# Bias of a two-layer kernel on Trainium2: column sums of w_out split between GpSimd and TensorE, one eviction of the result

## The chip, the cores and the metric

One core of a Trainium2 chip. The time is the device time of an execution in microseconds (us); executions of a kernel are compared with the executions of the kernel before in the same rounds on the same chip. Engines in the profile: PE is TensorE's matmuls, PEld its weight loads, DVE is VectorE, ACT is ScalarE, POOL is GpSimd, SP is SyncE.

## The reference

A spectral mixing layer (real FFT along 3008 positions, a complex 256x256 product with soft threshold, inverse FFT), then a two-layer network on 24064 tokens of width 256 with 2048 hidden units:

```python
h = x @ w_in
r = np.maximum(h, 0.0)
g = s * (r * r) + b
return (g @ w_out).astype(np.float32)
```

Since s and b are scalars, g @ w_out = s * (r*r @ w_out) + b * (column sums of w_out). Those column sums times b are the "bias": 256 numbers, wanted on all 128 partitions.

## The kernel before

It loads w_out as 16 blocks of 128 x 256 in f16 (one DMA from GpSimd's queue), adds the blocks two at a time on GpSimd in f32, folds the two halves, lets TensorE sum over the partitions with a matrix of ones, and lets ScalarE multiply by b and evict the result from PSUM twice, into the two halves of `bias_bc`:

```python
w_out_t = cpool.tile([P, MC, D], F16, name="w_out_t")
bias_bc = cpool.tile([P, 2, D], F32, name="bias_bc")
# ... cut
def sum_w_out():
    acc = opool.tile([P, 2, D], F32, name="acc", tag="ost")
    nc.gpsimd.tensor_tensor(out=acc, in0=w_out_t[:, 0:2], in1=w_out_t[:, 2:4], op=ALU.add)
    for q in range(4, MC, 2):
        nc.gpsimd.tensor_tensor(out=acc, in0=acc, in1=w_out_t[:, q : q + 2], op=ALU.add)
    nc.gpsimd.tensor_tensor(out=w_sum, in0=acc[:, 0], in1=acc[:, 1], op=ALU.add)

def make_bias():
    ps = other_bank()
    nc.tensor.matmul(ps[:, 0:D], ones, w_sum, start=True, stop=True)
    for j in range(2):
        nc.scalar.activation(out=bias_bc[:, j], in_=ps[:, 0:D], func=AF.Copy, scale=bb_bc)
```

The stage that runs meanwhile, and all the rest of the kernel, is this loop: first-stage products into two double banks `psh` (line 769), relu by ScalarE into `rt` (776), square mostly by VectorE into `gt` (783), second-stage products into `psa` (840), eviction with s and the bias by VectorE (850).

```python
nc.tensor.matmul(o, w_in_t[dc][:, mc * P : (mc + 1) * P], r, ...)              # 769
nc.scalar.activation(out=rt[:, :, 0:w], in_=ps[:, :, 0:w], func=AF.Relu)       # 776
nc.vector.tensor_tensor(out=gt[:, :, 0:w], in0=rt[:, :, 0:w], in1=rt[:, :, 0:w], op=ALU.mult)
nc.tensor.matmul(ps[0:size, h, :], gts[...][:, mc % 2, ...], w_out_t[:, mc, :], ...)   # 840
nc.vector.scalar_tensor_tensor(
    out=ost[0:size, 0:k], in0=ps[0:size, 0:k], scalar=s_bc[0:size],
    in1=bias_bc[0:size, 0:k], op0=ALU.mult, op1=ALU.add)                       # 850
# ... cut
plan.setdefault(15, []).append(make_bias)   # slot 15 of the first output tile
```

The framework that builds the kernel orders each engine's instructions by its own schedule, so a slot is a priority rather than a place.

## Time and profile before

| | before |
|---|---|
| median time | 847.02 us (3 runs, 846.86 to 847.43) |
| TensorE busy | 833.8 us, 99% of the span of 845.0 |
| VectorE, ScalarE, GpSimd busy | 82%, 76%, 5% |
| bias matmul at / w_sum ready at | 51.95 us / 50.0 us |
| TensorE's true idle time from 48 to 60 us, after 60 us | 0.84 us, 4.9 us |

How to read it: the busy share counts a matmul as busy for its whole latency (0.27 us for the bias matmul, whose successor starts 0.11 us after it), so it hides short waits. The last row is the idle time that the prediction works out from the matmuls' starts; it is what a smoother schedule could win.

### The profile page before, as it was taken

How to read it: one execution, taken by the hardware profiler on the slowest of the kernel's cores; microseconds unless marked ns; L12 is line 12 of the kernel's file. 1: busy time of each engine (PE TensorE's matmuls, PEld its weight loads, DVE VectorE, ACT ScalarE, POOL GpSimd, SP SyncE). 2: the span in 40 equal slices, each digit the busy share in tenths (PEclk: the TensorE clock that was granted, in tenths of full speed). 3: DMA queues.
4: the chain of work that ended last, by engine and by line, in shares of the span. 5: the costliest groups of instructions: out<-in, count | busy, mean ns of one | idle time of the engine just before them, and what ended most of it. 6: DMA issues, size and time to landing. Idle time of an engine off the chain costs nothing.

```text
span 845.0 us, 17114 instructions
## 1 busy us (share of the span) xinstructions
PE 833.8 (99%) x6653; PEld 599.6 (71%) x6653; DVE 693.6 (82%) x1026; ACT 641.8 (76%) x864; POOL 45.0 (5%) x71
## 2 busy tenths in 40 slices
PE   8999999999999999999999999999999999999997
PEld 6857767777677766777677776777667777766765
DVE  5989987888888987888888888798978888776674
ACT  5988887778778877787777787778877878766673
POOL 5331000000000001000000000000000000000000
PEclk9999999999999999999999999999999999999999
DMA  8945567124752367324761248513354223411111
GB/s 202 180 143 122 121 173 203 57 77 101 203 154 56 101 169 190 92 68 107 189 175 49 81 103 205 160 42 91 113 144 125 64 74 95 112 33 38 38 44 50
DMA packets 105746, 96.06 MB, mean 114 GB/s; under 512 B 9542, under 2 KB 97482, under 8 KB 104322
## 3 DMA queue, kind: packets, MB, share of 16 engines
q1 hardware_dynamic: 99218, 80.55, 33.0%
q0 software_dynamic: 6448, 14.42, 10.6%
q8 instruction: 52, 0.85, 0.4%
q14 instruction: 28, 0.23, 0.1%
HBM read 53.52 MB, written 46.66 MB: 119 GB/s over the span
## 4 chain that ended last, share of the span: by engine, by line
PE 90%; ACT 3%; DMA 3%; DVE 2%; issue 1%; POOL 0%; SPq 0%; ACTq 0%; DVEq 0%; POOLq 0%
PE psa L840 37%; PE psh L769 36%; PE psf L635 4%; PE psf L570 2%; PE psf L621 2%; PE psf L606 2%; PE psf L665 2%; PE psf L718 2%; ACT rt L776 2%; PE psm L426 1%; DMA x<-in_x_dram 1%; DMA ud<-u 1%; DVE gt L783 1%; DMA us<-ud 1%; DMA F_c<-dft_fwd 0%
## 5 line engine op out<-in xcount | busy, mean ns | idle before, releaser
L776 ACT ACTIVATE rt<-psh 128x1024 f32<-128x1024 f32 (+2 forms) x384 | 386.7, 1008 | 119.6 <-PE psh L769 117.5
L783 DVE TENSOR_TENSOR gt<-rt 128x1024 f16<-128x1024 f32 (+2 forms) x322 | 385.7, 1202 | 95.4 <-ACT rt L776 94.5
L840 PE MATMUL psa<-w_out_t,gt 128*128 128x256 f16 (+1 forms) x3024 | 454.4, 272 | 0.1
L840 PEld LDWEIGHTS <-gt 128*128 128x128 f16 (+1 forms) x3024 | 300.9, 101 | 187.0 <-issue 1.4
L769 PE MATMUL psh<-yt,w_in 128*128 128x512 f16 (+1 forms) x1344 | 396.3, 378 | 0.2 <-ACT rt L776 0.2
L769 PEld LDWEIGHTS <-w_in 128*128 128x128 f16 x1536 | 142.8, 98 | 27.3 <-issue 1.8
L850 DVE SCALAR_TENSOR_TENSOR ost<-psa,s_bc,bias_bc 128x512 f32<-128x512 f32 (+2 forms) x97 | 71.1, 733 | 10.0 <-PE psa L840 8.2
L780 ACT ACTIVATE gt<-rt 128x1024 f16<-128x1024 f32 (+2 forms) x62 | 65.3, 1054 | 1.0
L640 DVE TENSOR_TENSOR ring<-psf,s 128x512 f16<-128x512 f32 x84 | 57.5, 685 | 3.8 <-PE psf L635 3.3
L170 ACT CAST v<-psf 128x512 f16<-128x512 f32 x78 | 45.3, 583 | 19.7 <-PE psf L665 19.7
L170 ACT CAST xf<-psf 128x512 f16<-128x512 f32 x82 | 47.9, 586 | 10.9 <-PE psf L606 10.9
L170 ACT CAST u<-psf 96x512 f16<-96x512 f32 x76 | 43.9, 580 | 12.4 <-PE psf L570 12.2
L769 PE MATMUL psh<-tail,w_in 128*128 128x512 f16 (+1 forms) x192 | 52.1, 353 | 0.0
L635 PE MATMUL psf<-W_g,xf 128*128 128x256 f16 x336 | 50.4, 273 | 0.0
L170 ACT CAST yt<-psf 128x480 f16<-128x480 f32 (+2 forms) x73 | 37.8, 525 | 11.6 <-PE psf L718 11.6
L213 POOL DMA_DIRECT2D x<-in_x_dram x36 | 18.7, 526 | 430.3 <-PE psf L570 429.2
L570 PE MATMUL psf<-x,A_t 94*96 94x512 f16 x103 | 39.3, 382 | 1.1 <-ACT yt L170 0.5
L646 DVE TENSOR_TENSOR ring<-ring,high 128x512 f16<-128x512 f16 x84 | 35.6, 423 | 2.3
L647 DVE TENSOR_TENSOR ring<-ring 128x512 f16<-128x512 f16 x84 | 35.5, 423 | 2.0
L645 DVE TENSOR_TENSOR ring<-ring,low 128x512 f16<-128x512 f16 x84 | 35.4, 421 | 1.6
L635 PEld LDWEIGHTS <-xf 128*128 128x128 f16 x336 | 32.9, 98 | 3.8
L718 PE MATMUL psf<-C_t,vs 96*128 96x96 f16 x448 | 33.2, 205 | 0.2 <-ACT yt L170 0.2
(97 smaller groups left out, 499.5 us busy)
## 6 DMA issues: line engine op xcount, KB each, us to landing
out_dram<-ost SPq DMA_DIRECT2D x152, 128.0 KB
ud<-u SPq DMA_DIRECT2D x28, 384.0 KB
us<-ud SPq DMA_DIRECT2D x28, 384.0 KB
vd<-v SPq DMA_DIRECT2D x42, 256.0 KB
vs<-vd SPq DMA_DIRECT2D x14, 768.0 KB
x<-in_x_dram POOLq DMA_DIRECT2D x28, 376.0 KB, 5.9
ring<-ring SPq DMA_DIRECT2D x280, 32.0 KB
out_dram<-ost SPq DMA_DIRECT2D x16, 120.0 KB
```

Source lines behind the costliest of these rows:

```text
L170: return None, nc.scalar.copy(out=dst, in_=src)
L570: nc.tensor.matmul(ps[0:96, :], A_t[0:N1, :], x16[(b, c)][0:N1, j * D : (j + 2) * D], start=True, stop=True,)
L635: nc.tensor.matmul(ps[:, r, :], xt[:, 2 - r, dc], W_g[:, dc, r], start=(dc == 0), stop=(dc == DC - 1),)
L640: nc.vector.tensor_tensor(out=t, in0=ps, in1=hold[i // 2][:, i % 2].unsqueeze(1).to_broadcast([P, 2, D]), op=ALU.add,)
L646: nc.vector.tensor_tensor(out=m, in0=m, in1=high, op=ALU.min)
L718: nc.tensor.matmul(ps[:, j * 96 : (j + 1) * 96], vs[(b, h)][:, k, ec * P : (ec + 1) * P], C_t, start=True, stop=True,)
L769: nc.tensor.matmul(o, w_in_t[dc][:, mc * P : (mc + 1) * P], r, start=(dc == 0), stop=(dc == DC - 1),)
L776: nc.scalar.activation(out=rt[:, :, 0:w], in_=ps[:, :, 0:w], func=AF.Relu)
L780: nc.scalar.activation(out=gt[:, :, 0:w], in_=rt[:, :, 0:w], func=AF.Square)
L783: nc.vector.tensor_tensor(out=gt[:, :, 0:w], in0=rt[:, :, 0:w], in1=rt[:, :, 0:w], op=ALU.mult)
L840: nc.tensor.matmul(ps[0:size, h, :], gts[(ti, mc // 2)][:, mc % 2, sub * size : (sub + 1) * size], w_out_t[:, mc, :], start=(mc == 0), sto ...
L850: nc.vector.scalar_tensor_tensor(out=ost[0:size, 0:k], in0=ps[0:size, 0:k], scalar=s_bc[0:size], in1=bias_bc[0:size, 0:k], op0=ALU.mult, o ...
```

## The change

Its intent: a shorter sum on GpSimd, and one eviction fewer on ScalarE. GpSimd sums 12 of the 16 blocks and keeps the two halves apart; TensorE takes the four others and the two halves in one accumulation of six matmuls. The bias leaves PSUM once, and line 850 (854 in the new numbering; the lines shift by four) reads it with a broadcast. The load of w_out is cut in two, and the bias is planned one slot earlier.

```diff
-    bias_bc = cpool.tile([P, 2, D], F32, name="bias_bc")
+    bias_bc = cpool.tile([P, D], F32, name="bias_bc")
-        nc.gpsimd.dma_start(out=w_out_t, in_=moe_w_out.rearrange("(mc p) d -> p mc d", p=P))
+        for q in (slice(0, 12), slice(12, MC)):
+            nc.gpsimd.dma_start(out=w_out_t[:, q], in_=moe_w_out.rearrange(...)[:, q])
-    w_sum = cpool.tile([P, D], F16, name="w_sum")
+    w_sum = cpool.tile([P, 2, D], F16, name="w_sum")
-        for q in range(4, MC, 2):
+        for q in (4, 6, 8):
             nc.gpsimd.tensor_tensor(out=acc, in0=acc, in1=w_out_t[:, q : q + 2], op=ALU.add)
-        nc.gpsimd.tensor_tensor(out=w_sum, in0=acc[:, 0], in1=acc[:, 1], op=ALU.add)
+        nc.gpsimd.tensor_tensor(out=w_sum, in0=acc, in1=w_out_t[:, 10:12], op=ALU.add)
-        nc.tensor.matmul(ps[:, 0:D], ones, w_sum, start=True, stop=True)
-        for j in range(2):
-            nc.scalar.activation(out=bias_bc[:, j], in_=ps[:, 0:D], func=AF.Copy, scale=bb_bc)
+        parts = [w_out_t[:, q] for q in range(12, MC)] + [w_sum[:, 0], w_sum[:, 1]]
+        for i, part in enumerate(parts):
+            nc.tensor.matmul(ps[:, 0:D], ones, part, start=(i == 0), stop=(i == len(parts) - 1))
+        nc.scalar.activation(out=bias_bc, in_=ps[:, 0:D], func=AF.Copy, scale=bb_bc)
-                    in1=bias_bc[0:size, 0:k], op0=ALU.mult, op1=ALU.add,
+                    in1=bias_bc[0:size].unsqueeze(1).to_broadcast([size, k, D]), op0=ALU.mult, op1=ALU.add,
-    plan.setdefault(15, []).append(make_bias)
+    plan.setdefault(14, []).append(make_bias)
```

More of the change, by code (lines that the diff above doesn't have):

```diff
@@ L291, in emit_load_weights @@
             nc.gpsimd.dma_start(out=w_in_t[dc], in_=moe_w_in[dc * P : (dc + 1) * P, :])
-        nc.gpsimd.dma_start(
-            out=w_out_t, in_=moe_w_out.rearrange("(mc p) d -> p mc d", p=P)
-        )
+        for q in (slice(0, 12), slice(12, MC)):
+            nc.gpsimd.dma_start(
+                out=w_out_t[:, q], in_=moe_w_out.rearrange("(mc p) d -> p mc d", p=P)[:, q]
+            )
     neg_lam = cpool.tile([P, 1], F32, name="neg_lam")
@@ L342, in sum_w_out @@
         )
-        for q in range(4, MC, 2):
+        for q in (4, 6, 8):
             nc.gpsimd.tensor_tensor(out=acc, in0=acc, in1=w_out_t[:, q : q + 2], op=ALU.add)
-        nc.gpsimd.tensor_tensor(out=w_sum, in0=acc[:, 0], in1=acc[:, 1], op=ALU.add)
+        nc.gpsimd.tensor_tensor(out=w_sum, in0=acc, in1=w_out_t[:, 10:12], op=ALU.add)
     def make_bias():
         ps = other_bank()
-        nc.tensor.matmul(ps[:, 0:D], ones, w_sum, start=True, stop=True)
-        for j in range(2):
-            nc.scalar.activation(
-                out=bias_bc[:, j], in_=ps[:, 0:D], func=AF.Copy, scale=bb_bc
+        parts = [w_out_t[:, q] for q in range(12, MC)] + [w_sum[:, 0], w_sum[:, 1]]
+        for i, part in enumerate(parts):
+            nc.tensor.matmul(
+                ps[:, 0:D], ones, part, start=(i == 0), stop=(i == len(parts) - 1)
             )
+        nc.scalar.activation(out=bias_bc, in_=ps[:, 0:D], func=AF.Copy, scale=bb_bc)
     us = {}
```

## The prediction

> **What bounds the kernel now.** I read the page from the top: busy shares, the 40 slices, the chain that ended last. Then the timelines of TensorE, ScalarE and GpSimd around the only place where the changed lines run, 33 to 60 us.
>
> ```profile
> PE 833.8 (99%) x6653; PEld 599.6 (71%) x6653; DVE 693.6 (82%) x1026; ACT 641.8 (76%) x864; POOL 45.0 (5%) x71
> ...
> PE   8999999999999999999999999999999999999997
> ...
> POOL 5331000000000001000000000000000000000000
> PEclk9999999999999999999999999999999999999999
> ...
> PE 90%; ACT 3%; DMA 3%; DVE 2%; issue 1%; POOL 0%; SPq 0%; ACTq 0%; DVEq 0%; POOLq 0%
> ```
>
> TensorE is busy for 99% and is 90% of the chain; GpSimd, whose work the change mostly cuts, is 5% busy, over half of it (25.5 of 45.0 us) in the first 60 us, and 0% of the chain. A busy TensorE is not yet a full one, so I took every matmul's start and subtracted from each start-to-start distance the time that its columns need (columns / 2.4 GHz + 2.5 ns). What is left over is TensorE's true idle time: 10.3 us before 48 us, 0.84 us from 48 to 60 us, 4.9 us in the remaining 780 us, and after the last matmul some 4.4 us of last eviction and store. So from 48 us on only more or fewer matmul columns, or those 0.84 + 4.9 us, can move the end.
>
> GpSimd, with the column sums (start us, length us, engine, line, operation, tiles, count, idle before):
>
> ```profile
> 35.11 0.61 POOL L304 TENSOR_SCALAR high<-b_st 128x512 f16<-128x512 f32 x1
> 40.67 1.15 POOL L340 TENSOR_TENSOR acc<-w_out_t 128x512 f32<-128x512 f16 x1 [4.95 <-DMA w_out_t<-in_moe_w_out_dram]
> 41.90 7.30 POOL L344 TENSOR_TENSOR acc<-acc,w_out_t 128x512 f32<-128x512 f32 x6
> 49.28 0.72 POOL L345 TENSOR_TENSOR w_sum<-acc 128x256 f16<-128x256 f32 x1
> 62.65 0.96 POOL L209 COPY x<-us 1x1 f16<-1x1 f16 x4 [12.65 <-PE psh L769]
> ```
>
> It waits 4.95 us for the whole of w_out, adds for 9.3 us, and has w_sum at 50.0 us; then it has nothing to do for 12.65 us. The consumers, on TensorE and ScalarE:
>
> ```profile
> 49.62 0.38 PE L570 MATMUL psa<-x,A_t 94*96 94x512 f16 x1
> 50.17 1.94 PE L769 MATMUL psh<-yt,w_in 128*128 128x512 f16 x8 [0.17 <-ACT rt L776]
> 51.95 0.27 PE L349 MATMUL psa<-w_sum,ones 128*128 128x256 f16 x1
> 52.06 0.38 PE L840 MATMUL psa<-w_out_t,gt 128*128 128x256 f16 x2
> ```
>
> ```profile
> 51.38 1.96 ACT L776 ACTIVATE rt<-psh 128x1024 f32<-128x1024 f32 x2
> 53.20 0.49 ACT L351 ACTIVATE bias_bc<-psa,bb_bc 128x256 f32<-128x256 f32 x1
> 53.56 1.98 ACT L776 ACTIVATE rt<-psh 128x1024 f32<-128x1024 f32 x2
> 55.43 0.47 ACT L351 ACTIVATE bias_bc<-psa,bb_bc 128x256 f32<-128x256 f32 x1
> 55.79 1.94 ACT L776 ACTIVATE rt<-psh 128x1024 f32<-128x1024 f32 x2
> ```
>
> The bias matmul at 51.95 us has no bracket of idle time: w_sum had been ready for 1.95 us, so the sum delays nothing today. Bias_bc is complete at 55.9 us and first read by VectorE (the eviction of line 850) at 63.1 us: 7 us of slack. ScalarE is full from 49.1 to 57.7 us and holds TensorE up a little through the banks of psh: gaps of 0.33 us ahead of 50.17, 0.21 ahead of 52.48, and 0.05 to 0.09 us at four later points. One more thing: the program plans this bias in slot 15 of the first output tile, but its matmul ran after 16 of that tile's 32 first-stage matmuls, where TensorE was about to wait. The executed order is thus not the program's; small work is moved into gaps.
>
> **What the Trainium skill says.** "TensorE: Matmul & The Clock Gate", section "Wait — 56ns, not 53.3ns?", gives a warm matmul N / 2.4 GHz + about 2.5 ns, so 109 ns at 256 columns; in the trace the step from 51.95 to 52.06 is 0.11 us: they agree. "GPSIMD Engine Reference", section 3.1, gives about 2.6 cycles per element for a two-input add, at 1.2 GHz 1109 ns for 512 elements before dispatch; the trace has 1150 to 1154 ns, close, while its 256-element add, 724 ns, shows a larger fixed part (0.43 us for 256 more elements). "ScalarE: Activation LUTs", section "What ACT_TABLE_LOAD costs", gives 186 ns + 0.833 ns per element, some 93 ns more for a pointer operand, and 93 ns of overlap: 492 ns for the bias eviction; the trace has 492 and 468 ns, and 0.36 us from its start to the next one's. "VectorE: DVE Perf Modes", section "Why PSUM operands drop a tier", says a PSUM operand in fp32 stays at the 1x rate; line 850 already reads PSUM, so its now-broadcast second operand has no faster mode to lose.
>
> **The change part by part.**
> 1. GpSimd: eight adds become five (L340, three accumulating, one that writes both halves of w_sum as f16). Removed: three accumulating adds at 7.30 / 6 = 1.22 us and the 0.72 us fold, less one f16 add that replaces a fourth accumulation at about the same 1.2 us. 9.3 us become about 5 x 1.22 = 6.1 us. None of it is on the path: worth 0.
> 2. w_out's load in 12 + 4 blocks: the same bytes in two issues, perhaps 0.3 us more issuing on a GpSimd that waits there anyway. w_in, ahead on the same queue, takes a median 14.0 us and so lands near 33.5 us; w_out lands at 40.65; spread evenly, three quarters land at 33.5 + 0.75 x 7.1 = about 38.9 us (estimate). w_sum would then be ready near 38.9 + 6.1 = 45 us in place of 50. Worth 0 by itself, but the bias group can go into an earlier gap.
> 3. TensorE: one bias matmul becomes six (four blocks, two halves), all 256 columns wide on the unchanged `ones`: 5 x 0.109 = +0.55 us on the engine that sets the end, out of a total of about 823 us of columns (840.5 us to the last matmul, less the gaps and the first microsecond).
> 4. ScalarE: one bias eviction less, 0.36 us off an engine that is full just then. It shortens TensorE's waits for psh by at most that.
> 5. VectorE: L850's second operand repeats one row pair with a broadcast. L640 has just that form already (f32 PSUM operand plus an f32 tile broadcast over the middle dimension, 128x512), at 685 ns with an f16 output; L850 takes 733 with f32 output. So 0 for 97 instructions. If it cost even 0.1 us each, that were 9.7 us of an engine 82% busy, hidden mostly.
> 6. Memory: half of bias_bc saved, half a kilobyte more w_sum. No buffer count changes.
>
> Sum on TensorE: +0.55 us of columns. Against it stand the gaps that the group can fill: 0.44 and 0.68 us ahead of 45.34 and 46.20, 0.44 ahead of 47.68, 0.33 ahead of 50.17, 0.21 ahead of 52.48. If the six (0.65 us together) fall in one or two of these, about half to all is free, and 0.1 to 0.3 us of ScalarE relief comes on top. My net is 0.0 us, with -0.4 to +0.6 as the direct effect. **I choose 847.0 us**, the time of before.
>
> **The rivals.** (a) The bias was a wait for everyone and the change frees it: then some microseconds go. Against it: no idle bracket at L349, 0% POOL in the chain, 7 us slack before L850. Most it could give: the 0.84 us of gaps in 48 to 60 us, so 846.2. (b) The group is put into TensorE's order so early that it must wait on the chip for w_sum (in-order matmuls, everything behind it stalls). For it: the order is fixed before the run, the margin was 1.95 us, and w_sum's readiness is now an estimate near 45 us in a stage where TensorE has gaps. It would cost up to 1 to 2 us: 848 to 849. (c) The changed order ripples: a few swapped matmuls move evictions later on. The 4.9 us of later gaps, in single pieces up to 0.36 us, show how much there is to win, and a shift of a few of them gives +/- 1 us. (d) L850 slower by broadcasting: the pattern of L640 speaks against it; if VectorE did slow by 0.1 us per eviction, I would expect at most 1 to 3 us.
>
> **Range and chances.** The three runs of before spread over 0.57 us. Direct effect -0.4 to +0.6, ripple about +/- 1, with a tail upwards from (b): 845.9 to 848.4 us holds it 8 times in 10. Two per cent are 17 us, more than all TensorE gaps of the whole trace together (16.0 us): faster 0.003, within 98.9%, slower 0.008.
>
> **What would show it.** Right: 6 matmuls at the bias line, back to back at 0.11 us; one ScalarE eviction of about 0.48 us; five GpSimd adds ending near 45 us; L850's mean within 10 ns of 733; TensorE's gaps from 48 us on between 4.5 and 7 us. Wrong: a TensorE idle bracket on the bias line naming GpSimd's w_sum (rival b); L850 over 0.76 us (d); a time under 845.5 us, which would mean that the sum delayed the path in a way that I did not see; or over 849, a stall or a reordered stage later on.

## The result

The changed kernel took 848.08 us in the median (847.66 to 848.97, 6 runs), the kernel before in the same rounds 847.16 us (846.86 to 848.13, 6 runs): ratio 1.001, 95% interval 0.9997 to 1.0023. A ratio here is the mean time of one kernel's fast runs over that of the other's of the same rounds, so not quite the ratio of the medians. The times alone do not settle a sign. The traces do, as follows.

First the page of the changed kernel, its busy line and its chain (the lines that answer to those at the head of the prediction):

```profile
PE 833.6 (99%) x6658; PEld 599.7 (71%) x6658; DVE 693.6 (82%) x1026; ACT 641.6 (76%) x863; POOL 43.2 (5%) x69
...
PE 92%; ACT 3%; DVE 2%; DMA 1%; issue 1%; POOL 0%; ACTq 0%; DVEq 0%; POOLq 0%
```

Five matmuls more, one ScalarE and two GpSimd instructions fewer, and TensorE is as much the bound as it was. GpSimd's timeline (start us, length us, engine, line, operation, tiles, count, idle before):

```profile
40.60 1.15 POOL L343 TENSOR_TENSOR acc<-w_out_t 128x512 f32<-128x512 f16 x1 [4.57 <-DMA w_out_t<-in_moe_w_out_dram]
41.83 3.62 POOL L347 TENSOR_TENSOR acc<-acc,w_out_t 128x512 f32<-128x512 f32 x3
45.52 1.15 POOL L348 TENSOR_TENSOR w_sum<-acc,w_out_t 128x512 f16<-128x512 f32 x1
```

The sum is done at 46.67 us in place of 50.0. TensorE's and ScalarE's timelines where the bias is consumed:

```profile
50.49 1.94 PE L773 MATMUL psh<-yt,w_in 128*128 128x512 f16 x8 [0.17 <-ACT rt L780]
52.27 0.60 PE L354 MATMUL psa<-w_out_t,ones 128*128 128x256 f16 x4
52.80 1.94 PE L773 MATMUL psh<-yt,w_in 128*128 128x512 f16 x8
54.58 0.38 PE L354 MATMUL psa<-w_sum,ones 128*128 128x256 f16 x2
54.94 1.94 PE L773 MATMUL psh<-yt,w_in 128*128 128x512 f16 x8
56.71 0.49 PE L844 MATMUL psa<-w_out_t,gt 128*128 128x256 f16 x3
```

```profile
53.86 1.94 ACT L780 ACTIVATE rt<-psh 128x1024 f32<-128x1024 f32 x2 [0.20 <-PE psh L773]
55.70 0.47 ACT L357 ACTIVATE bias_bc<-psa,bb_bc 128x256 f32<-128x256 f32 x1
56.05 1.94 ACT L780 ACTIVATE rt<-psh 128x1024 f32<-128x1024 f32 x2
```

The bias group, split by the schedule into four matmuls and two, sits where before small second-stage matmuls sat: the two at 52.06 us that the prediction shows, and these, in the kernel before:

```profile
53.34 0.27 PE L840 MATMUL psa<-w_out_t,gt 128*128 128x256 f16 x1
54.31 0.49 PE L840 MATMUL psa<-w_out_t,gt 128*128 128x256 f16 x3
```

In the changed kernel none of those runs before 56.71 us. And there is a bracket of 0.20 us on ScalarE at 53.86 us: where a bias eviction stood before, it now waits a little for TensorE. The bracket does not come from the missing eviction: the trace of e11 below, which has both evictions, shows it as well (0.20 us at 53.44 us).

**Where the time went.** Both traces are so regular that they can be cut into three pieces: the start-up, up to the first forward-DFT matmul (psf<-g,F_t); part A, from there to the first psf<-W_t,xf matmul, some 49 us with the bias in it; and part B, on to the start of the last matmul. "Columns" is what the matmuls of part A need by the formula that the prediction uses (columns / 2.4 GHz + 2.5 ns; in these traces a matmul of 256 columns is followed 0.11 us later by the next, one of 512 after 0.22 us), "gaps" the rest.

| trace | start-up | part A | columns of A | gaps of A | part B |
|---|---|---|---|---|---|
| before | 16.39 | 48.88 | 43.87 | 5.02 | 775.24 |
| changed | 16.72 | 49.39 | 44.41 | 4.97 | 775.25 |

Part A grew by 0.51 us: five matmuls' columns, 0.55 us, less 0.04 us of gaps. Part B is the same to 0.01 us in this pair; between traces of one kernel it differs by about 0.1 us (e1 below). The other 0.33 us of this pair of traces lie in the start-up, ahead of every changed instruction.

### The profile page after: what moved, and what is told of

The parts are those of the page before. It is cut to its first block, busy times and chain, and to the rows that moved or that the text cites. A ratio compares the mean times of both kernels' runs of the same rounds, so it can differ in the third digit from the quotient of the medians.

```text
span 846.0 us, 17119 instructions
## 1 busy us (share of the span) xinstructions
PE 833.6 (99%) x6658; PEld 599.7 (71%) x6658; DVE 693.6 (82%) x1026; ACT 641.6 (76%) x863; POOL 43.2 (5%) x69
## 4 chain that ended last, share of the span: by engine, by line
PE 92%; ACT 3%; DVE 2%; DMA 1%; issue 1%; POOL 0%; ACTq 0%; DVEq 0%; POOLq 0%
PE psa L844 37%; PE psh L773 37%; PE psf L639 4%; PE psf L574 2%; PE psf L625 2%; PE psf L610 2%; PE psf L669 2%; PE psf L722 2%; ACT rt L780 1%; PE psm L430 1%; DMA x<-in_x_dram 1%; DMA F_c<-dft_fwd 1%; PE psf L460 0%; ACT yt L170 0%; DVE gt L787 0%
```

## The experiments

Twelve runs, all correct. The order of each was compared with that of its parent, engine by engine; "the same order" below means row for row.

**The same kernels again (two runs).** e1 is the changed kernel and e5 the kernel before, unaltered.

> The changed kernel once more, unaltered, with more rounds, to separate a fixed cost from the scatter of the start. I measure on the trace the stretch from the first forward-DFT matmul (psf<-g,F_t) to the start of the last matmul: 824.13 us before, 824.63 after; ahead of it lies the start-up, 16.39 us before and 16.72 after. Theory A (the five added matmuls' columns are paid in full, nothing else moved): stretch 824.6 +/- 0.1 again, ratio of times 1.0006, so a median 0.4 to 0.7 us over before; the start-up varies by some tenths for no reason of the change. Rival B (splitting the load of w_out slows the start): start-up is again 0.3 us longer than in the kernel before, the ratio 1.0010 or more.

> The kernel before, unaltered, profiled once more: the scatter of the start and of the stretch in the same program. Theory A: stretch 824.13 +/- 0.08; start-up anywhere from 16.2 to 17.0 us, moved by when the first loads land (F_c took 4.00 us to be there in the kernel before and 4.72 in the changed one). If the start-up is 16.39 +/- 0.05 once more, its 0.33 us in the changed kernel are not scatter.

Measured: e1 847.79 us (847.51 to 848.47, 5 runs) against 847.65 (847.05 to 848.15, 9 runs), ratio 1.0003, interval 0.999 to 1.0015. Its trace: start-up 16.39 us, part A 49.39, part B 775.36. e5's single run 847.46 us: start-up 16.71, part A 48.87, part B 775.24. So the start-up went the other way round in this pair: rival B falls, it is scatter. Over all fourteen traces it lies between 16.29 and 16.81 us; in the first pair it followed the landing of the F_c table (4.00 us on the chain of waits before, 4.72 us changed). Part A repeats to 0.01 us in both kernels. Part B does not quite: with e1's 775.36 us the whole stretch of e1 is 824.75 us, a little outside the 824.6 +/- 0.1 that I had expected. The change costs 0.51 us, 0.06%, between these traces; five rounds of whole-kernel times do not resolve that.

**One eviction alone (two runs).** The edit on the kernel before:

```diff
-    bias_bc = cpool.tile([P, 2, D], F32, name="bias_bc")
+    bias_bc = cpool.tile([P, D], F32, name="bias_bc")
-        for j in range(2):
-            nc.scalar.activation(out=bias_bc[:, j], in_=ps[:, 0:D], func=AF.Copy, scale=bb_bc)
+        nc.scalar.activation(out=bias_bc, in_=ps[:, 0:D], func=AF.Copy, scale=bb_bc)
-                    in1=bias_bc[0:size, 0:k], ...
+                    in1=bias_bc[0:size].unsqueeze(1).to_broadcast([size, k, D]), ...
```

> The kernel before with only the single eviction of the bias and the broadcast operand of line 850; sums and load as before. Theory A (TensorE's columns decide; ScalarE's 0.36 us fall into its own slack): stretch 824.0 to 824.1 us against 824.13, at most 0.15 us won in the gaps of 48 to 60 us. Rival C (ScalarE is what holds TensorE there, so the eviction saved is a gain that the added matmuls hid): stretch 823.8 or less, a gap of 0.2 us ahead of the next psh matmul gone. Line 850 stays within 10 ns of 733 ns in both; if it is over 760, the broadcast costs.

Measured: 847.62 us (5 runs) against 847.65, ratio 1.0001. TensorE's order differs from that of before in seven rows near 57 us. The trace gave neither theory: part A 49.37 us, half a microsecond longer than before, with the columns unchanged (43.87) and the gaps at 5.50. The new gap is at 60.33 us. The two timelines in question are GpSimd's and TensorE's:

```profile
48.17 2.38 POOL L344 TENSOR_TENSOR acc<-acc,w_out_t 128x512 f32<-128x512 f32 x2
50.63 1.75 POOL L345 TENSOR_TENSOR w_sum<-acc 128x256 f16<-128x256 f32 x1
```

```profile
60.33 0.39 PE L837 MATMUL psa<-w_out_t,gt 128*128 128x256 f16 x2 [0.29 <-DVE gt L780]
```

In this execution w_out happened to land 1.3 us later, so the last add, 0.72 us long in the kernel before, ran while VectorE had begun its products (first gt at 50.57 us): the add took 1.75 us and the second gt 1.75 us in place of 1.22. VectorE was then half a microsecond behind, and TensorE waited for a gt. That opened a new theory (F, below) and left the eviction undecided.

> The kernel of e2 once more, for a look without its accident: there w_out landed 1.3 us later than in the kernel before, the last GpSimd add (50.63 us) met VectorE's first two products gt, took 1.75 us in place of 0.72, one gt took 1.75 in place of 1.22, and TensorE stood 0.46 us at 60.3 us. I now cut the stretch at the first psf<-W_t,xf matmul: part A (some 49 us) is 48.88 and 48.87 us in two runs of before and 49.39 in two of the changed kernel. Theory A (ScalarE's saved eviction is worth next to nothing): if the sum is over before the first gt, part A is 48.80 to 48.90 us. Theory C (the saved eviction is a gain): 48.7 or less. If the sum again ends late, part A is again about 49.3 and says nothing of the eviction.

Measured: 846.97 us (one run); w_sum done at 50.01 us, first gt at 50.13; part A 48.89 us, against 48.88 and 48.87. The saved eviction is worth nothing here (+0.01 us; the order is that of e2). Line 850's 97 instructions have a median of 745 ns with the broadcast as without it, so the broadcast is free too.

**Two evictions in the changed kernel.** The converse: the changed kernel with the full `bias_bc`, two evictions, no broadcast; the order differs by that one eviction.

> The changed kernel with two evictions of the bias into a full bias_bc again and line 850 reading it without a broadcast, all else as changed; the built order differs by that one eviction. Theory A: part A 49.39 to 49.5 us, ScalarE's extra 0.36 us lies in its own slack. Theory C (the eviction saved paid for part of the added matmuls): 49.65 us or more.

Measured: 847.74 us (one run), part A 49.41 us against 49.39. Theory C falls from this side too: 0.36 us of ScalarE, in the stage where ScalarE is fullest, move part A by 0.02 us.

**The load of w_out (two runs).** e3 is the kernel before with only the load split in 12 + 4 blocks, e12 the changed kernel with the load whole. The order of the other engines is the same.

> The kernel before with only the load of w_out in 12 + 4 blocks. Theory A: stretch 824.1 +/- 0.1, start-up between 16.2 and 17.0 without a cause in the change. My prediction's step 2 said that the first three quarters land about 1.8 us before the rest; the changed kernel's trace shows its first add starting at 40.60 us against 40.67, with the issue 0.94 us later, so I now expect both parts to land within 0.5 us of each other, at about 20 us after the first issue. Rival B (the split delays the start or the later DMA): start-up of 16.7 or more and a stretch 0.2 us or more longer.

> The changed kernel with w_out loaded in one piece as before. The two parts land some 1.3 us apart (19.0 and 19.3 us after their issues at 21.6 and 22.6 us in the changed kernel; first add at 39.64 us in e3). Theory: the sum starts about 1 us later and ends near 47 to 48 us, still well before TensorE's w_sum matmuls at 54.3 us and before the first gt at 50.1 us; part A 49.39 +/- 0.03 us. Rival (the early landing is what the changed kernel lives on): part A over 49.6 us, with a wait ahead of the w_sum matmuls or a slowed gt.

Measured: e3 847.38 us (one run), part A 48.87; first part landed 19.2 us after its issue at 20.4, and the first add began at 39.64 us. e12 847.35 us (one run), part A 49.38; issue at 21.3, landing 20.3 us later, first add at 41.64, w_sum at 47.7. My expectation for e3, both parts within 0.5 us of each other, was wrong: with 19.5 us from an issue at 21.4 the second part landed about 1.3 us after the first. A lead of 1.3 us, then, of no use by itself: part A is the same with and without it.

**More matmuls.** The changed kernel with all 16 blocks on TensorE and no GpSimd sum:

```diff
-        parts = [w_out_t[:, q] for q in range(12, MC)] + [w_sum[:, 0], w_sum[:, 1]]
+        parts = [w_out_t[:, q] for q in range(MC)]
-                    sum_w_out()
```

> The changed kernel with all 16 blocks summed by TensorE (16 matmuls in place of 6) and no GpSimd sum at all. It doubles and more the suspected cost. Theory A: against the kernel before 15 more matmuls of 256 columns, 15 x 0.109 = 1.64 us; the gaps of 48 to 60 us are as little filled as in the changed kernel, so stretch 825.6 to 825.8, time 1.5 to 1.7 us over before. Rival D (matmuls added there fall into TensorE's waits for ScalarE and are nearly free, the changed kernel's excess came from elsewhere): stretch 824.6 to 825.0.

Measured: 848.57 us (848.46 to 848.78, 5 runs) against 847.65, ratio 1.0011, interval 0.9997 to 1.0025. Part A 50.36 us: 1.48 us over before, of 1.64 us of columns, so 0.16 us found a gap. By the traces theory A holds and rival D falls: in this place 90% of an added matmul is paid. In whole-kernel medians it is 0.9 us, less than the 1.5 expected, but the interval covers both.

**The bias in another place (three runs).** The edit is one number, `plan.setdefault(14, ...)` to 4 or 0. e6 and e8 are the changed kernel, e7 is e2's kernel with its 9.3 us sum in slot 4.

> The changed kernel with the bias group planned in slot 4 in place of 14. The built order then has the six matmuls ahead of the first psh matmul, among the last first-stage matmuls of batch 1, where TensorE has gaps of 0.68 and 0.44 us, and it no longer follows two full rounds of psh. Theory A with filling (matmuls cost nothing where the engine waits for an eviction anyway): of the 0.65 us of columns 0.3 to 0.6 fall into these gaps; stretch 824.0 to 824.3, that is 0.3 to 0.6 us under the changed kernel and about equal to before. Rival E (w_sum, at 46.7 us in the changed trace, is late there, or the bias eviction in the middle of the full ScalarE delays an eviction that TensorE waits for): stretch 824.6 or more, with idle time ahead of the bias line or of the matmuls behind it.

> The changed kernel with the bias group in slot 0: its first five matmuls stand ahead of the first L574 matmul of the last units, at about 46 us, where w_sum (46.7 us) is not yet there. Theory: the four block matmuls fill the 0.68 us gap, the w_sum ones wait 0.3 to 0.6 us; stretch 824.2 to 824.6, between e6 and the changed kernel. A stretch below e6's would say that the wait for w_sum is hidden too.

> The kernel before with the single eviction, its GpSimd sum of 9.3 us left whole, and the bias matmul planned in slot 4. The order then has the one bias matmul at about 46.5 us of the trace, but w_sum is ready at 50.0. This is my prediction's rival (b) made real. Expected: TensorE stands still for some 3.3 us ahead of the bias line, released by GpSimd, and does not win it back, since nothing behind it has that much slack: stretch 827.0 to 827.6, time 3 to 3.6 us over before. If TensorE regains it in later gaps, the stretch is under 825.5, and TensorE's total of columns isn't what sets the end.

Measured, e6: 847.48 us (847.04 to 849.47, 5 runs) against 847.16 (846.86 to 849.3, 9 runs), ratio 1.0. e8: 847.06 us (one run). Part A is 49.10 and 49.11 us, 0.29 us under the changed kernel and 0.22 over before: the columns are 44.41 as in the changed kernel, the gaps 4.69 in place of 4.97. The group did fill the 0.44 us gap that had stood ahead of 47.68 us. In the changed kernel that gap is here (the bracket shows 0.28 us of it):

```profile
48.00 0.38 PE L574 MATMUL psf<-x,A_t 94*96 94x512 f16 x1 [0.28 <-ACT u L170]
```

TensorE's timeline in e6, where the other three of the six stand between 46.79 and 47.34 us:

```profile
47.74 0.27 PE L354 MATMUL psa<-w_out_t,ones 128*128 128x256 f16 x1
47.85 0.38 PE L354 MATMUL psa<-w_sum,ones 128*128 128x256 f16 x2
48.06 0.38 PE L574 MATMUL psf<-x,A_t 94*96 94x512 f16 x1
48.33 1.89 PE L773 MATMUL psh<-yt,w_in 128*128 128x512 f16 x8
```

No bracket of idle time stands ahead of them. In e8 w_sum was ready at 45.86 us, ahead of the group at 46.10, so the wait of 0.3 to 0.6 us that I had expected there did not come. So the mechanism that I counted on exists, in a place where the change did not put the matmuls. The 826.21 us that e6's whole stretch took come from its profiled run alone (849.47 us, the slowest of its five): part B was 777.11 us with waits of up to 0.80 us for a load (us<-ud), while e8, nearly the same order, has 775.24. What delayed those loads in that execution is open; the kernel before also has one execution of 849.3 us among its nine.

e7: 853.29 us (852.34 to 854.38, 4 runs) against 847.16, ratio 1.007, interval 1.0056 to 1.0083: 6 us, where I had expected 3 to 3.6. TensorE's timeline, and busy time per stretch (stretch, its us, then busy us and count of PE, PEld, DVE, ACT, POOL, then the granted clock, DMA share, GB/s):

```profile
50.65 0.37 PE L349 MATMUL psa<-w_sum,ones 128*128 128x256 f16 x1 [4.14 <-POOL w_sum L345]
...
52.84 2.78 PE L766 MATMUL psh<-yt,w_in 128*128 128x512 f16 x8
```

```profile
46.00:50.60 4.60, 0.38 (x1) 0.10 (x1) 0.53 (x2) 0.46 (x2) 4.28 (x5) 0.70 0.00 0
50.60:52.80 2.20, 2.15 (x9) 1.18 (x9) 0.99 (x2) 1.53 (x3) 0.00 (x0) 0.50 0.00 0
52.80:55.40 2.60, 2.60 (x9) 1.06 (x8) 0.75 (x2) 1.11 (x3) 0.00 (x0) 0.65 0.51 150
55.40:58.00 2.60, 2.44 (x14) 1.07 (x12) 2.02 (x2) 2.60 (x4) 0.00 (x0) 1.00 0.00 2
```

The wait for w_sum is 4.14 us and drags ScalarE and VectorE down with it. And after it TensorE runs at half its clock (0.50) for some four microseconds: matmuls of 512 columns start 0.43 us apart in place of 0.22. The clock had fallen during the wait: a mean of 0.70 over the 4.60 us of the first row is 2.8 us at 0.50 and the rest at 1.00, so it fell at about 47.8 us; the 0.65 of the third row puts its return at about 54.6 us. That is the part that I had left out. Part A is 54.91 us, and nothing is won back: part B is 774.92 us, but only since it starts a few matmuls later in the order (0.32 us more columns in A).

**GpSimd against VectorE.** Four adds without use behind w_sum in the kernel before; the order of all other engines is the same.

```diff
         nc.gpsimd.tensor_tensor(out=w_sum, in0=acc[:, 0], in1=acc[:, 1], op=ALU.add)
+        for q in range(4, 12, 2):
+            nc.gpsimd.tensor_tensor(out=acc, in0=acc, in1=w_out_t[:, q : q + 2], op=ALU.add)
```

> The kernel before with four more adds of 128x512 on GpSimd behind w_sum, whose result nobody reads; the built order of every other engine is the same row for row. It makes the accident of e2 on purpose. Theory F (an add of GpSimd and a product of VectorE with two inputs in SBUF slow each other): the adds from 50.0 us on take 1.7 us or more in place of 1.15, three or four of the gt products take about 1.75 in place of 1.22, VectorE is 1.5 to 2.1 us behind and TensorE with it, part A 50.3 to 51.0 us. Rival (in e2 only the late w_sum did it, or VectorE has slack there): gt stays at 1.22 us or part A within 48.8 to 49.1 us.

Measured: 851.6 us (one run), part A 53.19 us, 4.3 us over before with the columns unchanged. VectorE's products at line 785 and GpSimd's adds, by source line:

```profile
L785 DVE TENSOR_TENSOR gt<-rt x322: 943/1222/2176, 50.2 to 838.7; 128x1024 f16<-128x1024 f32 x137, 128x960 f16<-128x960 f32 x13, 128x768 f16<-128x768 f32 x11
...
  PEld L842: 6.3, 7
  PE psa L842: 3.6, 4
  ACT rt L778: 2.5, 3
```

```profile
L347 POOL TENSOR_TENSOR acc<-acc,w_out_t x4: 2013/2018/2021, 50.9 to 57.2; 128x512 f32<-128x512 f32 x4
```

The three figures are the shortest, median and longest in ns; the three lines below the first are who waited for it (us, times). The adds took 2.02 us in place of 1.15, four gt 2.17 us in place of 1.22, and one more 1.74. That one, the first gt (at 50.21 us), was not met by an added add but by w_sum itself (50.13 to 50.86 us): the accident of e2 had come by itself once more, and is half a microsecond of the 4.3. The gt started 2.10 us apart, which is 1.14 us (their distance when alone) plus 0.96: the two engines take turns, an instruction at a time (adds start at 50.94, 53.04, 55.14 and 57.23 us, the gt between them at 51.87, 53.97, 56.06 and 58.16). Theory F holds: the four added adds cost 4 x 0.96 = 3.8 us where I had expected 1.5 to 2.1, since e2 had shown only one such meeting. This explains what the shorter sum is good for: in the kernel before it ends at 50.0 us and the first gt starts at 50.15; of the five other traces with the full sum and the bias in its old place, it ends 0.6 us (e5), 1.2 us (e3) and 0.1 us (e9) ahead of the first gt, and in e2 and e10 it met it. In the changed kernel the margin is 50.47 - 46.67 = 3.8 us. How often the kernel before loses its half microsecond that way, two traces in six cannot say. Where it does, its part A can be as long as the changed kernel's (49.37 us in e2 against 49.39), so the 0.51 us is the cost against an undisturbed execution, and the mean cost over many is not shown.

No version beat both kernels: the shortest part A with any edit (48.87 us in e3, 48.89 in e9) is that of before.

## Why the prediction was right or wrong

The range (845.9 to 848.4 us) held the time, 848.08. Point by point:

- **GpSimd (step 1): right.** Five adds from 40.60 to 46.67 us are 6.07 us, predicted 6.1, worth 0 on the path.
- **The load (step 2): the size was off.** Predicted 38.9 us for the first three quarters and w_sum at 45; measured 40.55 and 46.67. Half of that is the issue, which came 0.9 us later for reasons ahead of it; most of the rest is that the first part's lead over the second was some 1.3 us in e3, not 1.8. Nothing hung on it.
- **TensorE (step 3): right,** +0.55 us of columns. **The filling of gaps: mis-sized.** The prediction's sum said "about half to all is free" and came to 0.0 us net. It rested on one reading, that "small work is moved into gaps", drawn from where a single matmul stood. Measured, 0.04 us were free. The gaps that I had listed (0.44 and 0.68 us ahead of 45.34 and 46.20, 0.44 ahead of 47.68) lie ahead of the place where the group was put; the places it got, four matmuls ahead of 52.80 and two ahead of 54.94, not six back to back as I had named for a sign, were ones which second-stage matmuls had filled already, so they moved back. The gap ahead of the one place shrank from 0.21 to 0.09 us, and one of 0.14 us stood ahead of the other, where none had been. e6 and e8 show 0.29 us of filling once the group stands by a real gap.
- **ScalarE (step 4): mis-sized.** Predicted 0.1 to 0.3 us of relief; e9 and e11 measure 0.00 to 0.02. The likely reason stood in the profile: TensorE had other matmuls to do while it waited for psh.
- **VectorE and memory (steps 5 and 6): right,** 733 ns on average before and after.
- **Rival (b),** the stall, did not come; e7 made it real with the long sum, at 5.7 us on the traces in place of 1 to 2: 4.14 us of wait, and some 1.6 us more with the clock at 0.50 after it. **Rival (c),** the ripple of order, was given +/- 1 us; none shows: part B agrees to 0.01 us in the first pair, well within its scatter of 0.1, and apart from the edited instructions the built order differs only in some rows of TensorE between 52 and 60 us. **Rival (d)** fell by line 850's unchanged time. **Rival (a)** fell as told there.
- **What the prediction lacked:** the scatter of the start-up (16.29 to 16.81 us), which is as large as the effect, and the meeting of GpSimd's sum with VectorE's products.

With the terms as measured the sum would have been 847.0 + 0.5 = 847.5 us; the remainder to 848.08 is within the scatter of the runs (before alone: 846.86 to 848.13). That the range held the time so near its upper end is owed to its allowance for a ripple that did not come.

## What to carry to other kernels

On an engine as full as TensorE here, an added small matmul cost nearly all its columns unless it stood right where the engine waited; look up which waits are already filled by other work before calling a slot free. Moving work off an idle engine won nothing here, except that it ended sooner: check what its last instruction would meet if it ran late. When an effect is under a tenth of a per cent, cut the trace at fixed instructions and compare the pieces; here that resolved some 0.02 us in part A where five rounds of times resolved one microsecond. A trace is one execution, though: e2 took two of them to read.

## What the Trainium skill lacked or had wrong

- "SBUF — State Buffer", section "SBUF: two separate sides", says of the ports that GpSimd shares with VectorE that they are an exclusive lock, that a VectorE instruction with two SBUF inputs takes part, and that the loser blocks fully. The runs agree: adds of 1.15 us and products of 1.22 us took 2.02 and 2.17 us when they met (e10). What it lacks is the figure for a chain of both: one pair per 2.10 us, 0.96 + 1.14.
- "TensorE: Matmul & The Clock Gate", section "What's actually happening", gives half clock after an idle window of about 3.4 us. e7 agrees that a long wait (4.14 us) halves the clock, but not that 3.4 us must first pass without matmuls: by its granted clock the fall came at about 47.8 us, some 1.4 us after the columns of the last matmul (start 46.13 us, 0.22 us of columns). The clock was back at about 54.6 us, 6.8 us later, and the wait with its aftermath cost 5.7 us.
- No page that I read says what splitting a queued load gains in time to its first part; here 768 of 1024 KB were there 1.3 us ahead of the rest (e3), some 20 us after the issue. In the kernel before, w_out is the last 1024 of the 3552 KB that this queue was given from 17.46 us on (x 4 x 376, w_in 2 x 512), and by the DMA records the queue moved about 200 KB per us from 23 to 39 us; at that rate 256 KB take 1.3 us (estimate).
